# Earlier x loads, a larger planned landing margin and a replanned issue order in a fused attention and feed-forward kernel

## The chip, the cores and the metric

The kernel runs on one core of a Trainium2 chip. The metric is device time in microseconds (us), the median of several executions. The time is 2.2 to 2.3 us more than the span that the profile shows, so differences of spans and differences of times can be compared.

Words used below: TensorE (PE in the profile), ScalarE (ACT), VectorE (DVE), and the queue that sends all DMAs (SPq). A *visit* is one step of the attention part: eight score matmuls, and then two exponentials ("exps") of 128x1024 on ScalarE. There are 512 visits, so 1024 exps.

## The reference, cut to what matters

```python
# B, S, D, H = 1, 2048, 1024, 32; Dh = 32; F = 3584; bf16
def _A_ref(x, wq, wk, wv, wo):
    q = (x @ wq).reshape(B, S, H, Dh).transpose(0, 2, 1, 3)
    k = x @ wk                       # one K and one V head for 32 query heads
    v = x @ wv
    scores = jnp.einsum("bhqd,bkd->bhqk", q, k) * (Dh ** -0.5)
    o = jnp.einsum("bhqk,bkd->bhqd", _softmax(scores), v)
    return o.transpose(0, 2, 1, 3).reshape(B, S, H * Dh) @ wo

def _B_ref(x, w_gate, w_up, w_down):
    return (_sigmoid(x @ w_gate) * (x @ w_up)) @ w_down

h = x + _A_ref(_layernorm(x), wq, wk, wv, wo)
h2 = h + _B_ref(_layernorm(h), w_gate, w_up, w_down)
```

(Shortened from the reference, same arithmetic.)

## The kernel before

The kernel is one Python program that *plans* before it emits. Every instruction becomes an object with an engine, dependencies and an estimated duration; a list scheduler walks through estimated time and appends each object to its engine's list; the lists are then emitted in that order. So a number in the cost estimate changes no instruction's content, only where it stands. An engine takes its list in order, so an instruction whose input is late holds up what stands behind it: in the profile of before, a projection on TensorE that waited 2.37 us held up the scores behind it, and ScalarE then waited 3.15 us for them (both lines are in the prediction).

The parts that the change and the argument touch (cuts marked with `...`):

```python
XT = 1000.0
...
    # Plan.step: when the plan believes that a DMA has landed
    if o.nbytes:
        go = max(s + 1400.0, self.dma_free["sp"])
        self.dma_free["sp"] = go + o.nbytes / 280.0
        o.end = self.dma_free["sp"] + 900.0 + (PIECE if o.key.startswith("sl") else XT if o.key.startswith("xT") else 0.0)
...
    # 65 sets of 5 numbers; visit v uses KNOBS[v // WIN], WIN = 8: which class of work fills TensorE, and when
    KNOBS = [(4, 6, 0, 0, 2), (4, 7, 1, 0, 2), (0, 6, 0, 4, 2), ...]
...
    for ts in [[0], [1]] + [[t, t + 1] for t in range(2, NT, 2)]:      # x tiles of 128 rows, in pairs
        ...                                                           # statistics, then on VectorE:
        xnorm[t] = pl.op("dve", lambda xt=xt, sc=sc: DVE.tensor_scalar(
            out=xt, in0=xt, scalar1=sc, scalar2=None, op0=ALU.mult), [cen, sv[1]], ...)
        if 1 < ts[-1] < NT - 6:
            load_x([ts[-1] + 5, ts[-1] + 6], [xnorm[ts[-1]]])
...
    def dma_xT(t):                                                    # x tiles 2 to 15 are transposed by DMA
        xT_ev[t] = dma(lambda: SP.dma_start_transpose(
            out=xnT4[t // 4][:, :, (t % 4) * P:(t % 4 + 1) * P], in_=x_sb[:, t, :]), f"xT{t}", P * D * 5 // 2,
            [xnorm[t]], prio=0, occ=1330.0)
...
    # emit_S: the two exps of a visit
            exps[u] = pl.op("act", lambda slot=slot, pb=pb: ACT.activation(
                out=pslot(slot).rearrange("p (a b) -> p a b", a=2), in_=S_ps[:, pb:pb + 2, :],
                func=ACTF.Exp, scale=SCALE), [last] + free, prio=3, **t_act(1024))
...
    def flush_hT():                                                   # feed-forward input of row tile t
        while late_hT and (late_hT[0] < 2 or (late_hT[0] - 2) in gu_last):
            t = late_hT.pop(0)
            hT_ev[t] = dma(lambda t=t: SP.dma_start_transpose(
                out=hnT[:, t % 2, :, :], in_=hn[:, :]), f"hT{t % 2}", P * D * 5 // 2,
                [hnorm[t], gu_last.get(t - 2)], prio=0, occ=1330.0)
            ...
...
        # nothing else can start, by the plan: a matmul whose result nobody reads
        pl.op("pe", mm(F_ps[:, spare[0], 0:256], ident[:, :], kT4[:, 0:256], True, True), ...).tag = "dummy"
```

While ScalarE works on the exps, the plan gives TensorE the rest: P times V, the gate and up products (from `hnT`), the down products (from `zone`). The matmul with no reader is called a dummy below.

The softmax here doesn't subtract the row's maximum and nothing guards it: scores larger than these inputs give would overflow.

## Time and profile before

| | before |
|---|---|
| median of 3 runs | 1081.53 us (1080.90 to 1082.35) |
| execution that the profile shows | 1082.78 us, span 1080.5 us |
| exps | 1024, 969.2 us of ScalarE |
| last exp starts, from there to the end | 1014.18, then 66.3 us |

From the page, the engines' busy times and the costliest group (columns: line, engine, operation, out<-in with shapes, count, busy us and mean ns, idle us before and what ended it); then the window of the tail (length, busy us of TensorE, its weight loads, VectorE, ScalarE, GpSimd; clock; DMA share; GB/s):

```profile
PE 1045.8 (97%) x12803; PEld 483.2 (45%) x12972; DVE 902.7 (84%) x1750; ACT 1007.9 (93%) x1172; POOL 28.4 (3%) x58
...
L693 ACT ACTIVATE Pr<-S_ps 128x1024 bf16<-128x1024 f32 x1024 | 969.2, 1179 | 4.7 <-PE S_ps L401 4.5
```

```profile
1010.00:1081.00 71.00, 66.72 (x446) 30.57 (x451) 22.05 (x40) 11.29 (x16) 0.80 (x2) 1.00 0.79 207
```

The exps alone fill 969 of 1080 us, and of all that time only 4.5 us are waits for scores. Two engines with over 90% are no contradiction: TensorE is filled up with feed-forward work that could stand elsewhere, ScalarE cannot give anything away.

### The profile page before, as it was taken

To read this page: it belongs to the slowest core of one execution; us is meant where nothing else is said; L and a number is where in the kernel's file an instruction comes from. 1 tells how busy PE (TensorE), PEld (TensorE's weight loads), DVE (VectorE), ACT (ScalarE), POOL (GpSimd) and SP (SyncE) were. 2 spreads that over 40 slices of the span, in tenths; PEclk is the share of its full clock that TensorE was granted. 3 is DMA by queue.
4 is the path that set the end of the run, shared out by engine and by line. 5 is a ranking of instruction groups with operands and counts; after the bars stand their busy time and mean duration, and the time that the engine had idled before them with its cause. 6 is when DMAs were issued, how large, how long until landed. Compare 5 with 4: busy or idle time off the path is not lost.

```text
span 1080.5 us, 31405 instructions
## 1 busy us (share of the span) xinstructions
PE 1045.8 (97%) x12803; PEld 483.2 (45%) x12972; DVE 902.7 (84%) x1750; ACT 1007.9 (93%) x1172; POOL 28.4 (3%) x58
## 2 busy tenths in 40 slices
PE   9999999999999999999999999999999999999998
PEld 6664444444444444444444444444444444444443
DVE  8789989898988889898888889898898989898721
ACT  6899999999999999999999999999999999999610
POOL 2100000000000000000000000000000000000000
PEclk9999999999999999999999999999999999999999
DMA  9997799927969597939659697987969596876994
GB/s 223 177 300 236 184 290 258 280 66 217 243 174 243 148 277 186 288 85 288 159 142 223 165 280 139 258 201 179 236 151 274 120 279 165 229 201 167 281 269 109
DMA packets 309359, 226.60 MB, mean 210 GB/s; under 512 B 121824, under 2 KB 300512, under 8 KB 309216
## 3 DMA queue, kind: packets, MB, share of 16 engines
q1 hardware_dynamic: 307136, 224.46, 81.3%
q8 instruction: 102, 1.67, 0.7%
q10 hardware_dynamic: 2080, 0.13, 0.1%
q14 instruction: 41, 0.34, 0.1%
HBM read 194.12 MB, written 7.86 MB: 187 GB/s over the span
## 4 chain that ended last, share of the span: by engine, by line
PE 77%; ACT 11%; DVE 5%; issue 5%; DMA 2%; SPq 0%; POOL 0%; DVEq 0%; ACTq 0%
PE F_ps L401 64%; PE S_ps L401 13%; ACT Pr L693 9%; DVE Ts L727 2%; DMA ring<-in_A_x_dram 1%; ACT tnh L968 1%; DVE st L338 1%; DVE st L340 1%; DMA zone<-ring 1%; DVE Rc L786 0%; DVE ring L385 0%; DVE hst L972 0%; DVE hact L287 0%; DVE Ts L734 0%; DVE ring L378 0%
## 5 line engine op out<-in xcount | busy, mean ns | idle before, releaser
L693 ACT ACTIVATE Pr<-S_ps 128x1024 bf16<-128x1024 f32 x1024 | 969.2, 1179 | 4.7 <-PE S_ps L401 4.5
L727 DVE TENSOR_TENSOR Ts<-Ts,Pr 128x1024 bf16<-128x1024 bf16 x736 | 482.5, 677 | 33.6 <-ACT Pr L693 31.7
L401 PE MATMUL F_ps<-ring,hnT 128*128 128x512 bf16 (+1 forms) x2005 | 411.8, 380 | 13.1 <-issue 9.6
L401 PEld LDWEIGHTS F_ps<-ring,hnT 128*128 128x128 bf16 (+1 forms) x2089 | 153.3, 97 | 192.3 <-issue 47.3
L401 PE MATMUL F_ps<-zone,hact 128*128 128x512 bf16 (+1 forms) x1153 | 212.1, 380 | 9.0 <-issue 8.2
L401 PE MATMUL S_ps<-QTb,kT 32*128 32x256 bf16 x4096 | 208.8, 273 | 1.1
L401 PEld LDWEIGHTS S_ps<-QTb,kT 32*128 32x128 bf16 x4096 | 64.1, 92 | 209.1 <-ACT Pr L693 143.5
L401 PE MATMUL F_ps<-Pr,Vb 128*32 128x256 bf16 x4096 | 135.3, 274 | 0.3 <-issue 0.3
L968 ACT ACTIVATE tnh<-F_ps 128x512 f32<-128x512 f32 x112 | 83.0, 742 | 43.1 <-PE F_ps L401 43.0
L401 PEld LDWEIGHTS F_ps<-zone,hact 128*128 128x128 bf16 (+1 forms) x1214 | 80.0, 97 | 92.7 <-issue 22.7
L727 DVE TENSOR_TENSOR Ts<-Pr 128x1024 bf16<-128x1024 bf16 x128 | 87.3, 684 | 39.9 <-ACT Pr L693 39.8
L972 DVE SCALAR_TENSOR_TENSOR hst<-tnh,F_ps 128x512 bf16<-128x512 f32 x112 | 76.6, 684 | 43.9 <-PE F_ps L401 40.8
L401 PEld LDWEIGHTS F_ps<-Pr,Vb 128*32 128x32 bf16 x4096 | 97.6, 96 | 30.2 <-issue 17.6
L401 PE MATMUL F_ps<-zone 128*128 128x256 bf16 (+5 forms) x639 | 74.9, 271 | 4.7 <-DMA zone<-ring 2.4
L401 PE MATMUL F_ps<-wo_sb,OT 128*128 128x512 bf16 (+1 forms) x289 | 61.5, 380 | 1.8 <-issue 1.4
L401 PEld LDWEIGHTS F_ps<-zone 128*128 128x128 bf16 (+1 forms) x646 | 43.6, 98 | 26.9 <-issue 7.6
L734 DVE TENSOR_TENSOR Ts<-Ts 128x1024 bf16<-128x1024 bf16 x64 | 44.0, 688 | 1.3
L1002 DVE SCALAR_TENSOR_TENSOR h_sb<-F_ps,h_sb 128x512 bf16<-128x512 f32 x32 | 21.8, 682 | 22.3 <-PE F_ps L401 22.1
L352 POOL TENSOR_SCALAR zb<-mvb 128x1 bf16<-128x1 bf16 (+1 forms) x25 | 10.3, 411 | 997.9 <-DVE mvb L348 997.9
L401 PEld LDWEIGHTS F_ps<-wo_sb,OT 128*128 128x128 bf16 (+1 forms) x304 | 22.4, 97 | 28.0 <-issue 7.0
L771 DVE COPY Oc<-F_ps 128x256 f32<-128x256 f32 x60 | 25.2, 420 | 7.4 <-PE F_ps L401 6.6
L776 DVE TENSOR_TENSOR Oc<-F_ps,Oc 128x256 f32<-128x256 f32 x60 | 25.4, 423 | 4.8 <-PE F_ps L401 3.2
(60 smaller groups left out, 333.2 us busy)
## 6 DMA issues: line engine op xcount, KB each, us to landing
ring<-in_B_w_gate_dram SPq DMA_DIRECT2D x314, 256.0 KB, 4.3
ring<-in_B_w_up_dram SPq DMA_DIRECT2D x310, 256.0 KB, 4.6
zone<-in_B_w_down_dram SPq DMA_DIRECT2D x28, 256.0 KB, 4.0
h_sb<-in_A_x_dram SPq DMA_DIRECT2D x16, 256.0 KB, 4.8
out_dram<-h_sb SPq DMA_DIRECT2D x32, 128.0 KB, 3.0
ring<-in_A_x_dram SPq DMA_DIRECT2D x7, 512.0 KB, 5.4
QTb<-q_scratch SPq DMA_DIRECT2D x14, 256.0 KB, 4.8
Pr<-in_B_w_up_dram SPq DMA_DIRECT2D x14, 256.0 KB, 4.4
```

What stands on the lines that cost most here:

```text
L338: a = pl.op("dve", lambda k=k, src=src: DVE.bn_stats(st[:, k, 0, :], src[:, 0:512]), dep, prio=prio, occ=590, lat=756, order=[st_user.get(k)])
L340: b = pl.op("dve", lambda k=k, src=src: DVE.bn_stats(st[:, k, 1, :], src[:, 512:1024]), dep, prio=prio, occ=590, lat=756, order=[st_user.g ...
L352: f = pl.op("pool", lambda: POOL.tensor_scalar(out=zb[:, ph, sl].unsqueeze(2), in0=mvb[:, ph, sl, 1:2], scalar1=LN_EPS_BF16, scalar2=None, ...
L401: fn = lambda: PE.matmul(o, lhsT=l, rhs=r, start=start, stop=stop, **kw)
L693: exps[u] = pl.op("act", lambda slot=slot, pb=pb: ACT.activation(out=pslot(slot).rearrange("p (a b) -> p a b", a=2), in_=S_ps[:, pb:pb + 2 ...
L727: o = pl.op("dve", lambda T=T, a=a, b=b: DVE.tensor_tensor(out=T, in0=a, in1=b, op=ALU.add), deps, prio=4, **t_dve(1024, 1.92))
L734: merge_ev[G] = pl.op("dve", lambda T4=T4: DVE.tensor_tensor(out=T4[:, :, 0, :], in0=T4[:, :, 0, :], in1=T4[:, :, 1, :], op=ALU.add), [sum ...
L771: oc_ev[G] = pl.op("dve", lambda: DVE.tensor_copy(out=Oc[:, :], in_=O), [last, o_ev.get(G - 1)], prio=0, **t_dve(256))
L776: a = pl.op("dve", lambda: DVE.tensor_tensor(out=Oc[:, :], in0=O, in1=Ob, op=ALU.add), [last, oc_ev[G], o_ev.get(G - 1)], prio=0, **t_dve( ...
L968: tanh_of[n] = pl.op("act", lambda: ACT.activation(out=tnh[:, n % 2, :], in_=F_ps[:, b, :], func=ACTF.Tanh, scale=0.5), [last, tn_user.get ...
L972: e = pl.op("dve", lambda: DVE.scalar_tensor_tensor(out=hst[:, n % NST, :], in0=tnh[:, n % 2, :], scalar=1.0, in1=F_ps[:, b, :], op0=ALU.a ...
L1002: e = pl.op("dve", lambda: DVE.scalar_tensor_tensor(out=h_sb[:, t % 4, sl], in0=F_ps[:, b, :], scalar=0.5, in1=h_sb[:, t % 4, sl], op0=ALU ...
```

## The change

Its intent: get x tiles 10 to 15 normalized sooner, and make the plan allow more time for the transposes of x to land, so that no projection stands in TensorE's list ahead of its data. The sets of KNOBS are new as well, so the order of work changes all through the kernel.

```diff
-XT = 1000.0
+XT = 1300.0
...
-    KNOBS = [(4, 6, 0, 0, 2), (4, 7, 1, 0, 2), (0, 6, 0, 4, 2), (1, 5, 0, 1, 2), ...
+    KNOBS = [(0, 6, 0, 2, 3), (1, 7, 1, 2, 1), (0, 5, 0, 4, 2), (3, 4, 0, 1, 2), ...
...
-            if 1 < ts[-1] < NT - 6:
-                load_x([ts[-1] + 5, ts[-1] + 6], [xnorm[ts[-1]]])
+            for k in {3: [8, 10], 5: [12], 7: [14]}.get(ts[-1], []):
+                load_x([k, k + 1], [xnorm[ts[-1]]])
```

## The prediction

> **What bounds the kernel now.** I read four things in order: the page, the waits of ScalarE by stretch, the busy time by window, and the timeline around the one large gap.
>
> The page calls TensorE 97% busy and ScalarE 93%. The share that matters is that of each stretch, so next come the windows (columns: stretch, length, busy us of each engine with instruction counts, granted clock, DMA share, GB/s):
>
> ```profile
> 36.00:42.30 6.30, 6.27 (x133) 4.55 (x125) 5.46 (x16) 6.04 (x9) 0.93 (x2) 1.00 1.47 198
> 42.30:47.80 5.50, 3.13 (x42) 2.01 (x39) 3.99 (x14) 2.35 (x4) 0.93 (x2) 0.77 0.84 176
> 47.80:53.00 5.20, 5.20 (x101) 3.79 (x99) 2.90 (x8) 4.86 (x6) 0.00 (x0) 0.92 0.22 47
> 60.00:120.00 60.00, 57.52 (x796) 29.57 (x802) 57.86 (x119) 60.00 (x67) 1.28 (x2) 1.00 0.76 234
> 120.00:1010.00 890.00, 866.08 (x10734) 384.16 (x10886) 777.50 (x1469) 890.00 (x1020) 16.35 (x28) 1.00 0.82 208
> ```
>
> The reader should see: from 60 to 1010 us ScalarE (fourth busy figure) works 950 of 950 us, and its list of waits in that stretch is empty. So the attention part, 1024 exps of 128x1024, is ScalarE without a gap. TensorE fills in feed-forward work there and has 26 us to spare. After the last exp comes a tail of 67 us on TensorE alone. The end is therefore: the moment from which ScalarE no longer waits, plus a fixed pile of ScalarE work, plus the tail. Only the first 60 us have waits of ScalarE to take away. They are (waits of ScalarE, 13 to 60 us: total, times, longest):
>
> ```profile
> ACT Pr L693 <- PE S_ps L401: 4.5, 5, 3.2
> ACT kT L286 <- PE F_ps L401: 1.3, 1, 1.3
> ```
>
> The 3.2 us is one gap. The timeline round it, 41.9 to 48.5 us:
>
> ```profile
> 42.31 0.24 PE L401 MATMUL F_ps<-zone 128*128 128x32 bf16 x3
> ...
> 44.92 2.21 PE L401 MATMUL F_ps<-zone 128*128 128x256 bf16 x25 [2.37 <-DMA zone<-ring]
> ...
> 47.06 0.61 PE L401 MATMUL S_ps<-QTb,kT 32*128 32x256 bf16 x8
> ...
> 47.73 1.02 ACT L693 ACTIVATE Pr<-S_ps 128x1024 bf16<-128x1024 f32 x1 [3.15 <-PE S_ps L401]
> ```
>
> TensorE reaches the K projection of x tiles 10 and 11 at 42.55 us (44.92 less 2.37) and waits for the DMA transposes of these tiles. The scores after them come late, and ScalarE runs dry for 3.15 us. The chain that ended last shows what these transposes hang on:
>
> ```profile
> 24.87 4.29 DMA ring<-in_A_x_dram
> ...
> 35.23 4.08 DMA ring<-in_A_x_dram
> 39.31 5.47 DMA zone<-ring
> 44.92 2.21 PE F_ps L401 x25
> ```
>
> The x load of tiles 14 and 15, sent at 35.23, is in flight in front of the transposes of tiles 10 and 11, sent at 37.92 and 39.31. Those took 6.1 and 5.5 us from issue to landing; the median of all 14 is 3.7.
>
> **What the Trainium skill says.** "Perfetto Trace Analysis", section Optimization Strategy: within a regime, find the gaps on the engine that should be saturated and what they wait for, since a kernel can have several regimes. That is the reading above. The trace agrees that there are regimes: ScalarE 890 of 890 us in the middle, 11 of 71 in the tail.
>
> "TensorE: Matmul & The Clock Gate", section The HAM clock gate: after an idle window of about 3.4 us the array runs at half clock until it has been busy for about as long. The trace agrees in kind: the granted clock is 0.56 between 44.9 and 47.8 us and 0.80 from 47.8 to 50, against 1.00 elsewhere. The gap was shorter (2.37 us) than the page's window, so the number is not borne out. The cost: the 25 matmuls at 44.92 are 8 of 256 columns (0.11 us each), 16 of 32 (0.03) and one more, 1.5 us at full clock, and took about 2.15 (47.06 less 44.92). The wait and the slow clock thus cost about 3 us before the next scores.
>
> "DMA: Bandwidth & Descriptors", section Issuing engines are not separate DMA queues: transfers interleave on the same 16 engines whoever issues them. Nothing in the trace speaks against it: landings of the same transposes range from 3.1 to 6.1 us.
>
> **The change part by part.**
>
> *The loads.* Before, the loads of tiles 8/9, 10/11, 12/13, 14/15 went out at 17.81, 24.87, 29.60, 35.23, each after the normalization of pair 2/3, 4/5, 6/7, 8/9. Now 10/11 follows 8/9 at once (about 18.4, one issue of 0.58 later), and 12/13 and 14/15 take the places at about 24.9 and 29.6. The place at 35.23 is empty. This takes 0.6 us of issue and 512 KB of transfer from in front of the transposes of 10/11. VectorE waited for x four times in that stretch (0.71, 0.38, 0.72, 0.77 us); the last three, 1.9 us, should go. So these transposes should be sent near 36.5 to 37.5 and land by 41 at the median time, by 43 at the worst seen.
>
> *Evacuations.* Comparing the instruction orders, four 256-column evacuations (one of Q, three to hact) pass from ScalarE to VectorE. On ScalarE each holds up the next exp by about 0.27 us (hact at 25.45, exp at 25.72): 1.1 us less there. On VectorE they cost 4 x 0.42 = 1.7 us, about what the earlier loads give it.
>
> *Dummies.* The larger margin makes the plan put 14 dummy matmuls, not 9, before the first projection from DMA transposes (tiles 2/3). That projection did not need even nine: its transposes, sent at 14.53 and 15.9, landed by 19.9 (4.0 us at most) and the dummies ran from 20.05. Five more at 0.11 are 0.55 us of new delay. Ten dummies are new in the whole kernel; the other five (before 6, now 11) are in the stretch where ScalarE is the bound, where 0.5 us of TensorE's 26 spare is free.
>
> *Order.* I summed TensorE's work from the first dummy in both orders, with 0.11 us for 256 columns, 0.0605 for 128, 0.03 for 32, 0.335 for one visit of scores and 1.86 for one PV pair with its sums (all from the timeline). To the end of score visit 11 (from 0): 20.86 us before. The trace has it at 42.31, so the sum plus 20.05 plus 1.40 of small waits. With the same 1.4 to 1.5: the new order ends visit 11 at 43.2 (sum 21.72). The projection of 10/11 now stands behind more Q work: sum 22.38, so 43.9, after the landing even at its worst. Visit 12 ends at 20.05 + 23.60 + 1.5 = 45.15 and its exp starts 0.12 later, at 45.3. Before it was 47.73. **Gain: 2.4 us.** (ScalarE will be waiting then: from the first exp of visit 3, at 23.63 + 0.55, its 18 exps of visits 3 to 11 at 0.93, seven evacuations at 0.27 and some 0.84 of K and V take 19.5 us, to 43.7. So a gap of about 1.6 us remains.)
>
> From there ScalarE needs 1.87 us a visit (9 exps in 8.52 us, 0.934 each). Visits 14 and 15 end at 27.48 and 29.68 in the sum, 2.2 apart, because two PV pairs stand between: about 0.6 us of new gaps there, against 0.25 before. Net **2.1 us**. Projections 12/13 and 14/15 come at sums of 29.68 and 31.36, near 51.3 and 53.1; their transposes should land near 47 and 51.
>
> *The rest.* Before the last exp both kernels have 1024 exps and 102 tanhs on ScalarE, after it ten tanhs. After the last scores TensorE's list is the same, row by row. The new order numbers move feed-forward work about behind ScalarE and cannot shorten it; TensorE's changes of mode are 1043 against 1042. Sum: 1081.5 - 2.1 = **1079.4 us**.
>
> **The rivals.** (a) *The whole stall comes back*: 3.15 us of gap plus the 1.1 us of moved evacuations, less 0.55 of dummies: 3.7 us, 1077.8. For it: the wait is on the chain that ended last, and my 1.4 us of small waits may shrink. Against it: TensorE was busy 6.27 of 6.30 us before the stall, so ScalarE's saved time only shows as its own waiting. (b) *The wait moves*: VectorE, with 1.7 us more to evacuate, normalizes tiles 12 to 15 as late as before (14/15 finished at 50.3) and TensorE waits at 53.1 instead. Before, their transposes landed at 56.6. A stall of 2 to 3 us there gives everything back: 1081.5. Against it: two of VectorE's waits of 47 to 49 us (1.47, 0.71) were consequences of the stall itself, so it should finish near 46 to 48. (c) *The replanned middle opens gaps on ScalarE*: 64 sets of numbers changed. For it: feed-forward groups now stand elsewhere among the score visits. Against it: not one gap in 950 us before. It would cost 1 us or so, 1080.5. (d) *Nothing on the path*: if the small dummies and gaps eat the gain, 1081.5.
>
> **Range and chances.** Rival (a) sets the lower end, at 1077.6 with 0.2 for run scatter; (b) and (d) the upper, 1081.4. The three times of before lie 1.4 us apart, so a median can shift by about 0.5. A change of 2% is 21.6 us; the first 60 us hold only about 6 us of ScalarE waits, and losing 21.6 us would need gaps in a middle that has none. Faster by over 2%: 0.005; slower: 0.01; within: 0.985.
>
> **What would show each step right or wrong.** Right: no wait of TensorE for the transposes near 42 to 45 us, and the clock at 1.00 there; the longest wait of ScalarE for scores near 1.5 to 2 us and not 3.2; visit 12's exp near 45.3; 14 dummies that end after the transposes have landed; ScalarE still 890 of 890 us from 120 to 1010. Wrong: a new wait for transposes at 53 us, a clock below 1 in the first 60 us after the start-up, or any wait of ScalarE after 60 us.

## The result, and the profile after

| | before | after |
|---|---|---|
| median of 4 runs, same chip | 1081.27 us (1080.90 to 1082.35) | 1081.83 us (1081.35 to 1082.98) |
| ratio | | 1.0005 (95%: 0.9988 to 1.0022) |
| profiled execution | 1082.78 us, span 1080.5 | 1081.35 us, span 1079.1 |

A ratio here and below is the mean time of one kernel's fast runs over that of the other's of the same rounds, so it is not quite the ratio of the medians. The time is the same; 1079.4 and the range 1077.6 to 1081.4 were both too low. Note the trap in the last row: the two profiles differ by 1.4 us in favour of after, but before's was a slow execution of its kernel and after's the fastest of its four.

The same windows of after as the prediction shows of before:

```profile
36.00:42.30 6.30, 6.30 (x132) 4.62 (x130) 6.09 (x18) 5.56 (x8) 0.93 (x2) 1.00 0.99 151
42.30:47.80 5.50, 5.50 (x117) 4.00 (x116) 4.26 (x15) 5.47 (x7) 1.32 (x2) 1.00 1.11 184
47.80:53.00 5.20, 5.01 (x140) 3.69 (x128) 1.53 (x3) 4.82 (x7) 0.00 (x0) 1.00 0.78 181
60.00:120.00 60.00, 59.88 (x803) 28.55 (x802) 57.95 (x119) 60.00 (x67) 1.60 (x2) 1.00 0.78 237
120.00:1010.00 890.00, 886.32 (x10846) 384.32 (x10844) 777.19 (x1467) 889.19 (x1019) 15.90 (x28) 1.00 0.80 207
```

In the second row the stall is gone: TensorE 5.50 of 5.50 us (3.13 before), ScalarE 5.47 (2.35 before), clock 1.00 (0.77 before). In the last row ScalarE, whose list of waits had been empty there, is 0.81 us short of 890. (TensorE's larger busy figures are no finding: the trace of before has 12803 matmuls for 12972 weight loads, so 169 records are missing. The second profile of before, told of below, has all of them, and there TensorE is busy 59.00 of 60 and 887.78 of 890 us in the last two rows. So the "26 us to spare" of the prediction are about 3: TensorE too is nearly full, and a late input on it soon reaches ScalarE.) The waits of ScalarE, first from 13 to 60 us, then from 60 to 1010:

```profile
ACT Pr L693 <- PE S_ps L401: 2.0, 5, 0.6
ACT kT L286 <- PE F_ps L401: 1.9, 1, 1.9
```

```profile
ACT Pr L693 <- PE S_ps L401: 0.8, 1, 0.8
```

Waits for scores fell from 4.5 to 2.0 us, the wait for the first projection grew from 1.3 to 1.9 (the added dummies), and one new wait of 0.8 us stands where before had none. The timeline around it in after (start, length, engine, operation, count, what ended the idle time before it):

```profile
162.73 1.04 PE L401 MATMUL F_ps<-ring,hnT 128*128 128x512 bf16 x4
...
165.90 1.30 SPq L877 DMA_TRANSPOSE hnT<-hn  x1
...
168.27 1.06 PE L401 MATMUL F_ps<-Pr,Vb 128*32 128x256 bf16 x32
169.26 0.28 PE L401 MATMUL F_ps<-kT,ident 128*128 128x256 bf16 x1
170.46 0.60 PE L401 MATMUL F_ps<-ring,hnT 128*128 128x512 bf16 x2 [0.93 <-DMA hnT<-hn]
171.00 0.40 PE L401 MATMUL S_ps<-QTb,kT 32*128 32x256 bf16 x8
171.45 1.94 ACT L693 ACTIVATE Pr<-S_ps 128x1024 bf16<-128x1024 f32 x2 [0.81 <-PE S_ps L401]
```

and the same change of row tiles in before:

```profile
168.97 1.23 SPq L877 DMA_TRANSPOSE hnT<-hn  x1
...
169.01 1.25 PE L401 MATMUL F_ps<-ring,hnT 128*128 128x512 bf16 x5
...
173.49 0.28 PE L401 MATMUL F_ps<-kT,ident 128*128 128x256 bf16 x1
173.83 0.38 PE L401 MATMUL F_ps<-ring,hnT 128*128 128x512 bf16 x1
```

`F_ps<-ring,hnT` is gate and up work (L877 sends the transpose). Before, that work of the previous row tile lasts until 170.26; the next tile's transpose is sent at 168.97, lands 3.8 us later at 172.8, and its first matmul at 173.83 waits for nothing. After, the previous tile's gate and up work is used up at 163.8, two us *before* the transpose is sent (165.90). It lands 4.5 us later, at 170.4. Down products, P times V and dummies (`F_ps<-kT,ident`) bridge the 6.7 us between the two tiles, all but 0.93 us, and the scores that stand behind that wait in TensorE's list come 0.81 us late for ScalarE.

One more wait stands in this profile and is easily missed, because the view names another releaser. It is at the projection of x tiles 14 and 15:

```profile
53.28 1.54 PE L401 MATMUL F_ps<-zone 128*128 128x256 bf16 x25 [0.47 <-DVE kT L287]
...
55.20 7.46 ACT L693 ACTIVATE Pr<-S_ps 128x1024 bf16<-128x1024 f32 x8 [0.37 <-PE S_ps L401]
```

The transpose of tile 15 was sent at 48.14 and landed at 53.15, 0.13 us before these matmuls began, and ScalarE waits 0.37 us for the scores behind them. This is rival (b) of the prediction, at the place that it named ("TensorE waits at 53.1 instead").

**A ledger.** Because ScalarE is the bound, the start of its Nth exp is a clock for progress, as long as the same other work lies between two counts (between the 41st and the 171st exp both kernels have ten tanhs). Counting exps in the first profile of each kernel gives:

| start of exp | 7th | 25th | 41st | 171st | last | span |
|---|---|---|---|---|---|---|
| before, us | 23.64 | 47.73 | 63.03 | 187.05 | 1014.18 | 1080.5 |
| after, us | 24.05 | 44.98 | 60.70 | 185.55 | 1012.74 | 1079.1 |
| after less before | +0.4 | -2.75 | -2.3 | -1.5 | -1.4 | -1.4 |

By this table the gain of the first 60 us was 2.3 us (2.1 was predicted), 0.8 was lost again near 171 us, and the rest reached the end. That would be 1.4 us in time. The timed runs show no gain at all. So either part of the table is not typical, or the timed runs hide something.

### The profile page after: what moved, and what is told of

Same layout as the page of the kernel before. It is cut to its first block, busy times and chain, and to the rows that moved or that the text cites. A ratio compares the mean times of both kernels' runs of the same rounds, so it can differ in the third digit from the quotient of the medians.

```text
span 1079.1 us, 31547 instructions
## 1 busy us (share of the span) xinstructions
PE 1068.4 (99%) x12955; PEld 484.4 (45%) x12955; DVE 903.6 (84%) x1754; ACT 1007.3 (93%) x1168; POOL 28.3 (3%) x58
## 4 chain that ended last, share of the span: by engine, by line
PE 93%; ACT 3%; DVE 2%; DMA 2%; issue 1%; SPq 0%
PE F_ps L401 77%; PE S_ps L401 15%; ACT Pr L693 3%; DMA zone<-in_A_wq_dram 1%; DMA zone<-ring 1%; DMA hnT<-hn 0%; DVE st L338 0%; DVE st L340 0%; ACT tnh L968 0%; DVE Ts L727 0%; DVE ring L385 0%; DVE ring L378 0%; SPq L302 0%; DVE mv L342 0%; DVE h_sb L1002 0%
## 5 line engine op out<-in xcount | busy, mean ns | idle before, releaser
L401 PE MATMUL F_ps<-ring,hnT 128*128 128x512 bf16 (+1 forms) x2110 | 428.4, 380 | 3.5 <-issue 2.1
L401 PE MATMUL F_ps<-zone,hact 128*128 128x512 bf16 (+1 forms) x1166 | 223.1, 380 | 0.2 <-issue 0.2
L972 DVE SCALAR_TENSOR_TENSOR hst<-tnh,F_ps 128x512 bf16<-128x512 f32 x112 | 76.4, 682 | 43.3 <-PE F_ps L401 41.7
L401 PE MATMUL F_ps<-zone 128*128 128x256 bf16 (+4 forms) x646 | 74.6, 270 | 1.0 <-DVE kT L287 0.5
L401 PE MATMUL F_ps<-wo_sb,OT 128*128 128x512 bf16 (+1 forms) x304 | 64.7, 380 | 0.0
```

The source lines that it names most:

```text
L401: fn = lambda: PE.matmul(o, lhsT=l, rhs=r, start=start, stop=stop, **kw)
L972: e = pl.op("dve", lambda: DVE.scalar_tensor_tensor(out=hst[:, n % NST, :], in0=tnh[:, n % 2, :], scalar=1.0, in1=F_ps[:, b, :], op0=ALU.a ...
```

## The experiments

First theory (H1): the stall at tiles 10 and 11 is a property of the kernel before, and its gain is given back by the new gap near 171 us and by dummies. Rival (H2): the profile of before shows an unusually bad execution; the usual stall is smaller, so less was ever there to win. Rival (H3): the loads do nothing, the new order does it all.

Experiments edit either kernel as text, or change its finished lists after planning, so that nothing else moves. All 18 runs gave correct results.

### The two kernels once more

No edit. Before (`e1_before_again`), and two looks at it later on another occasion; after (`e1_after_again`, and `e4_after_beside` beside other runs).

> The kernel before, unchanged, for a second profile and more times. Theory A (the profiled execution of before was an unusual one: its span of 1080.5 us is 1.5 us above what its median time leaves; the stall for the transposes of tiles 10/11 is shorter in a usual execution): a span near 1079 us here, and the gap of ScalarE near 45 us well under 3.15 us, at most 1.5 to 2. Theory B (the stall is always there and the new plan gives its gain back later): the gap again 3.0 to 3.3 us and the last exp again near 1015.3 us.

> The changed kernel, unchanged, for a second profile and more times; ratio to before 0.999 to 1.001. Theory A: no stall near 42 to 45 us, ScalarE's waits in the first 60 us about 4 us in all as in the first profile, one gap of about 0.8 us near 165 us at the transpose of the normalized rows. Theory B: gaps of ScalarE after 60 us of 2 us or more in all.

> The changed kernel once more, for comparison on this chip: ratio to before 0.9990 to 1.0010, gap of ScalarE of 0.8 us near 171 us, 25th exp between 44.8 and 46.0 us.

> A third profile of the kernel before, for the stall alone. If the first profile was the odd one: gap of ScalarE near 45 us of 1.2 to 2 us, clock 1.00 there, 25th exp near 46.0. If the two profiles are two equal cases: either is as likely, the 25th exp at 46.0 or at 47.7.

> A fourth profile of the kernel before: as for the third, gap of 1.2 to 2 us and the 25th exp near 46.0 if the first was the odd one.

Times: before again 1081.93 against 1082.07 for before in the same rounds (ratio 0.9998, 0.9986 to 1.0011); after 1082.33 against the same 1082.07 (1.0000, 0.9987 to 1.0012), and 1082.34 against 1081.54 on another occasion (1.0001, 0.9989 to 1.0014). The looks took 1081.67 and 1080.25 (state unknown).

TensorE's wait for tiles 10 and 11 and the exps after it, in the second, third and fourth profile of the same kernel before, one fence each:

```profile
44.06 1.54 PE L401 MATMUL F_ps<-zone 128*128 128x256 bf16 x25 [1.50 <-DVE st L340]
45.98 2.85 ACT L693 ACTIVATE Pr<-S_ps 128x1024 bf16<-128x1024 f32 x3 [1.40 <-PE S_ps L401]
```

```profile
44.74 1.54 PE L401 MATMUL F_ps<-zone 128*128 128x256 bf16 x25 [1.95 <-DMA zone<-ring]
46.67 1.94 ACT L693 ACTIVATE Pr<-S_ps 128x1024 bf16<-128x1024 f32 x2 [1.84 <-PE S_ps L401]
```

```profile
43.30 1.54 PE L401 MATMUL F_ps<-zone 128*128 128x256 bf16 x25 [0.69 <-DVE st L338]
45.23 3.77 ACT L693 ACTIVATE Pr<-S_ps 128x1024 bf16<-128x1024 f32 x4 [0.59 <-PE S_ps L401]
```

The 25 matmuls took 1.54 us each time, so the array was at full speed, against 2.21 us in the first profile. Together (with the start of the Nth exp):

| profile | wait | granted clock, 44 to 48 us | 25th | 41st | 171st | last | span |
|---|---|---|---|---|---|---|---|
| before, first | 2.37 | 0.66 | 47.73 | 63.03 | 187.05 | 1014.18 | 1080.5 |
| before, second | 1.50 | 1.00 | 45.99 | 61.08 | 185.10 | 1012.25 | 1079.5 |
| before, third | 1.95 | 1.00 | 46.67 | 61.76 | 185.79 | 1012.92 | 1079.4 |
| before, fourth | 0.69 | 1.00 | 45.23 | 60.33 | 184.35 | 1011.49 | 1078.0 |
| **mean of before** | 1.63 | | 46.41 | 61.55 | 185.57 | 1012.71 | |
| after, three profiles | none | 1.00 in the first | 44.88 to 45.04 | 60.58 to 60.86 | 185.27 to 185.65 | 1012.46 to 1012.85 | 1078.8 to 1079.2 |
| **mean of after** | 0 | | 44.97 | 60.71 | 185.49 | 1012.68 | |

H2 is right, and H1 is right in its second half. The 25th exp of before lies anywhere between 45.23 and 47.73 us; the first profile is the worst of four. On average the gain at the 25th exp is 1.44 us, at the 41st 0.84. From the 41st to the 171st before took 124.02 us in all four profiles, after 124.85, 124.79 and 124.69: 0.76 lost, in each of the three. ScalarE does the same exps and the same ten tanhs there, busy 124.02 us in before and 124.04 in the first profile of after; the difference is the gap of 0.81. What is left is 0.08 us at the 171st exp and 0.03 at the last: by these means, 0.84 less 0.76 is nothing. The 0.84 rests on four profiles of before with a standard deviation of 1.1 us at the 41st exp, so its standard error is about 0.6 (an estimate from these profiles); the balance says where time was won and lost, not that it is zero to a tenth.

Why only 0.84 of 1.44 reaches the 41st exp can be read from more profiles. The kernels of `e2_hold_wd`, `e3_swap_hT` and `e4_early_norm`, told of below, differ from after only near 160 us and later. In their profiles the transpose of tile 15 lands at 50.6 to 51.4 us, nothing waits at 53 us, and from the 25th to the 41st exp they take 15.14 to 15.15 us. In the three profiles of after it lands at 53.0 to 53.3, TensorE waits 0.46 to 0.59 us, and the same stretch takes 15.71 to 15.83. Before takes 15.09 (15.30 in its first profile). So the wait at 53 us, and hardly anything else, costs these 0.6 us, and it too differs between executions: these three profiles have the 25th exp at 45.91, 45.48 and 44.85 and the 41st at 61.06, 60.62 and 59.99. Over all six the 41st is at 60.63, a gain of 0.9.

The clock tells how common the worst case is. Each run's record has the mean granted clock over the whole span. Both profiles here in which the clock fell near 45 us, this first one and one told of below, show 0.998 there; the other profiles show 1.00. Of 45 runs of before with a recorded clock, 9 have 0.998, and in one set of nine these are the four slowest (1082.69 to 1083.01 against 1080.98 to 1082.27). Of 14 such runs of after, none has. So the prediction was built on an event of about one run in five. (That the other eight fell at the same place was not looked at.) The clock is not the only source of scatter: in another set of nine no run has 0.998, and its slowest, 1083.46 and 1083.70, show 1.00. The profiles show two more. From the start of the last exp to the end it is 66.3 to 66.5 us in most, but 67.2 in the second of before; and from the 171st to the last exp the first profile of `e1_loads_moved`, next, took 827.80 us where two more of the same kernel took 827.14 and 827.18, with no wait in it.

### The loads alone, and the loads undone

`e1_loads_moved` is before, with only the three loads put where the changed kernel has them; all other lists are untouched. `e1_loads_back` is after with the loads put back.

```diff
 # loads_moved, after planning of before
+        rest = []
+        for i, o in enumerate(lists["sp"]):
+            if o is at["x8"]:
+                rest += [at["x8"], at["x10"]]
+            elif i == old["x10"]:
+                rest.append(at["x12"])
+            elif i == old["x12"]:
+                rest.append(at["x14"])
+            elif i != old["x14"]:
+                rest.append(o)
+        lists["sp"] = rest
+        at["x10"].deps, at["x12"].deps, at["x14"].deps = [xnorm[3]], [xnorm[5]], [xnorm[7]]
```

> Before, with only the x loads moved: every other instruction on every engine stands where it stood. Theory A: the transposes of 10/11 land in time; the time falls by what the usual stall costs, 0.5 to 1.5 us, ratio 0.9986 to 0.9995. Theory B: the time falls by 2.5 to 3.7 us, ratio 0.9966 to 0.9977. A third possibility, that the load was not what delayed the transposes: no change, and the stall still there.

> The changed kernel with its x loads put back to the places of before and every other instruction where it stands in the changed kernel. If the loads are what the change lives from: a stall for transposes near 44 us or later returns and the time rises by 1 to 3 us over the changed kernel. If the new order by itself already asks for the transposes late enough (about 1.4 us later than before): no rise, within 0.5 us of the changed kernel.

To see whether what the first run showed holds, two more looks were taken at the first:

> Before with only the loads moved, a second profile. If the load in front delays the transposes: TensorE waits 0.9 us or less for tiles 10/11 and the 25th exp comes by 45.5 us, in this and the next profile. If the wait only varies by execution: it may be anything from 0.7 to 2.4 us, the 25th exp from 45.2 to 47.7.

> A third profile of the same kernel, with the same two readings: wait of 0.9 us or less and the 25th exp by 45.5 us if the load is the cause, anything up to 2.4 and 47.7 if not.

With the loads moved alone, the line that read 2.37, 1.50, 1.95 and 0.69 us of wait reads, in the three profiles:

```profile
43.41 1.54 PE L401 MATMUL F_ps<-zone 128*128 128x256 bf16 x25 [0.67 <-DVE kT L287]
```

```profile
43.27 1.54 PE L401 MATMUL F_ps<-zone 128*128 128x256 bf16 x25 [0.67 <-DVE kT L287]
```

```profile
43.59 1.54 PE L401 MATMUL F_ps<-zone 128*128 128x256 bf16 x25 [0.68 <-DVE kT L287]
```

The wait is 0.67 us three times out of three. (The name behind the arrow is the releaser that the profile saw last; in all seven profiles of the old order the projection starts 0.1 to 0.2 us after the second transpose lands, so that is what it waits for.) The 25th exp is at 45.20 to 45.52, mean 45.35: 1.05 us sooner than the mean of before. Three against four is little, since the fourth profile of before has 0.69 too; but in the 15 profiles with early loads, of whatever kernel, the second transpose landed at 42.8 to 44.2 us, mean 43.3, and in the five with late ones at 43.2 to 45.0, mean 44.3. H3 falls: the loads bring the landing forward by about 1 us, though it still scatters. From the 41st exp to the 171st the kernel takes 124.01 to 124.12 us, as before, so the loads open no gap. The time, 1081.14 against 1082.07, ratio 0.9995 (0.9981 to 1.0008), cannot prove a gain of a thousandth.

Loads back in after: 1084.48 us, ratio 1.0024 (1.0012 to 1.0037), the one clear rise, and the 25th exp at 47.59. I had expected the old wait to return. Another came instead; TensorE's and ScalarE's waits, 13 to 60 us:

```profile
PE F_ps L401 <- DVE hact L287: 1.9, 2, 1.7
```

```profile
ACT hact L286 <- PE F_ps L401: 2.1, 2, 1.6
```

TensorE waits for an evacuation to `hact` by VectorE, and ScalarE for TensorE. The timeline of the same kernel shows what VectorE did:

```profile
29.43 0.69 DVE L338 BATCH_NORM_STATS2 st<-ring 128x6 f32<-128x512 bf16 x1 [1.99 <-DMA ring<-in_A_x_dram]
...
31.37 0.41 DVE L287 CAST hact<-F_ps 128x256 bf16<-128x256 f32 x1
...
31.83 1.05 PE L401 MATMUL F_ps<-zone 128*128 128x256 bf16 x8 [1.66 <-DVE hact L287]
```

VectorE waits 1.99 us for an x load, and the evacuation, one of those that the new order gives it, stands behind the statistics of that tile. So the new order needs the early loads; it is not an alternative to them.

### The dummies

`e2_no_fill` is after without its first group of added dummies, the 14 before the first projection; `e2_moved_no_fill` is before with the loads moved and without its nine; `e4_best_beside` is the same kernel again on another occasion.

```diff
+        fill = [o for o in lists["pe"] if o.tag == "dummy"][20:]
+        at = lists["pe"].index(fill[0])
+        drop = [o for i, o in enumerate(fill) if lists["pe"].index(o) == at + i]
+        lists["pe"] = [o for o in lists["pe"] if o not in drop]
```

> The changed kernel without the 14 dummy matmuls ahead of the first projection from DMA transposes; all else in place. Theory (the dummies only hold TensorE up, since the transposes of tiles 2/3 land by 19.9 us and the dummies end near 21.5): the first exp of visit 3 comes 1.2 to 1.5 us sooner (from 24.05 to about 22.7), and the 41st exp 0.8 to 1.4 us sooner (from 60.70), so 1080.5 to 1081.2 where the changed kernel has 1081.8. Rival (the next wait takes the gain: transposes of 10/11 or VectorE): visit 3 sooner, but the 41st exp at 60.5 or later, no change of the time. A drop of the clock below 1 in the first 40 us would be a third way to lose it.

> Before with the loads moved and without its nine dummies there. Same theory: visit 3 sooner by about 0.9 us; but this order asks for the transposes of 10/11 at 42.5 already and gets them at 43.3, so most of it becomes a longer wait there: 41st exp within 0.3 us of 60.43, time as e1_loads_moved.

> Before with the loads moved and without its nine dummies, the fastest so far, again: 0.9975 to 0.9995 of before, no gap of ScalarE after 60 us, last exp near 1011.5. If its first result was luck: ratio 0.9995 or more.

Without the dummies in after, the 7th exp comes 1.14 us sooner (22.91). Of that 0.2 is left at the 25th (44.78). The 41st is 0.77 sooner (59.93), but 0.57 of it is the wait at 53 us, which this profile does not have, as three with the dummies do not; one of those has its 41st at 59.99. So the dummies held TensorE up, and almost nothing came of their removal. The 171st comes at 185.68, no sooner than in after. TensorE's wait for the transposed `hnT`, and ScalarE's waits after 60 us:

```profile
PE F_ps L401 <- DMA hnT<-hn: 1.2, 1, 1.2
```

```profile
ACT Pr L693 <- PE S_ps L401: 1.4, 2, 1.1
```

The gaps had been 0.8 in all and are now 1.4: what was ahead at the 41st exp was waited for later. Time 1081.88 against 1082.27 (0.9998, 0.9986 to 1.0011).

Before with early loads and without dummies has no gap after 60 us and the earliest last exp of its call, 1011.49. It took 1080.10 us against 1082.27, ratio 0.9980 (0.9968 to 0.9993): the best figure of all, where I had expected that of the loads alone. But its last exp comes no sooner than in the fourth profile of before, also 1011.49. It was not repeated on the other occasion: 1081.15 against 1081.54, 0.9993 (0.9980 to 1.0005), inside the range that I had given for it, but with the last exp at 1013.61. There its profile shows the old trouble:

```profile
44.35 1.79 PE L401 MATMUL F_ps<-zone 128*128 128x256 bf16 x25 [1.90 <-DMA zone<-ring]
```

with a granted clock of 0.64 from 44 to 48 us. Without dummies TensorE reaches the projection a little sooner (44.35 less 1.90 is 42.45 us, against 42.6 to 42.9 with them) and again finds the transposes under way; the second was sent at 39.65, later than in the three profiles with the loads alone (38.60 to 39.10), and landed at 44.22. Two of its ten runs have a mean clock of 0.998.

### The gap near 171 us

Is it the traffic of the down weights, the place of the transpose in the queue, or the moment at which VectorE finishes `hn`? Three edits of after, and the last of them together with the removed dummies:

```diff
 # hold_wd: the next load of down weights waits until hnT has landed
+        first = next(o for o in lists["sp"][at:] if o.key.startswith("wd"))
+        first.deps.append(hT_ev[1])
 # swap_hT: hnT is sent one place sooner in the queue
+        sp[at - 1], sp[at] = sp[at], sp[at - 1]
 # early_norm: VectorE normalizes hn ahead of sums and one product, and the swap
+        lists["dve"] = [o for o in dv[:end] if o not in held_back] + [hnorm[1]] + held_back + dv[end + 1:]
+        sp[at - 1], sp[at] = sp[at], sp[at - 1]
```

> The changed kernel, with the eight weight loads that follow the transpose of the second tile's normalized rows (sent at 165.9 us) held until it has landed. If these loads slow the transpose (4.5 us to landing, median 3.1): it lands by 169.5, the gap of ScalarE of 0.8 us near 171 us goes, the 171st exp comes 0.7 to 0.9 us sooner (from 185.55), and the time falls by 0.5 to 0.9 us. If they do not: gap and time as in the changed kernel.

> The changed kernel, where the transpose of the second tile's normalized rows goes out just before the feed-forward transpose that stood in front of it, not just after. If that neighbour delays it (sent at 164.65 and 165.90, landing 4.4 to 4.8 us after the sending): it lands within 3.6 us, the wait of TensorE for it and the gap of 0.8 us on ScalarE near 171 us go, the 171st exp comes near 184.8 and the time falls by 0.5 to 0.9 us. If it lands no sooner, neither neighbour is the cause and it stays open.

> The changed kernel, where VectorE normalizes the second tile's rows ahead of three exp sums and one feed-forward product that stood before it, and their transpose is sent first. If the wait near 170 us is what takes the gain: the transpose is sent near 164.7 instead of 165.9, ScalarE's gap of 0.8 us goes, the 171st exp comes 0.6 to 0.9 us sooner (near 184.8) and the last exp too (near 1012.0), the time 0.6 to 0.9 us under the changed kernel of this job. If ScalarE loses the time anyway (another wait takes its place): the 171st exp stays near 185.6.

> The same, without the 14 dummies as well. Without them alone the 41st exp came 0.8 us sooner and the 171st not at all. If the wait near 170 us absorbed it: the 171st exp now near 184.0 to 184.4, last exp near 1011.4, time 1.2 to 1.7 us under the changed kernel of this job. If the tile's normalization cannot come sooner still: 171st exp as in e4_early_norm.

Holding the weights back did not help: TensorE waits 1.1 us for `hnT`, which took 4.7 us to land; 1081.97 against 1082.27 (0.9995, 0.9982 to 1.0007). Nor did the place in the queue: 1.1 us, 4.6 us to land; 1081.24 against 1081.40 (0.9997, 0.9984 to 1.0011). The early normalization did: sent at 163.88, landed 3.0 us later. The matmul that had waited 0.93 us, and ScalarE's waits after 60 us:

```profile
169.52 0.59 PE L401 MATMUL F_ps<-ring,hnT 128*128 128x512 bf16 x2
```

```profile
ACT Pr L693 <- PE S_ps L401: 0.2, 1, 0.2
```

So the cause of the gap is shown: the late `hn`. Yet the time stayed, 1081.70 against 1081.54 (0.9997, 0.9985 to 1.0010), and 41st to 171st exp took 124.92 us, no less than in after. (Against the changed kernel of the same occasion, 1082.34, the median is 0.64 us lower, as expected; the ratios to before, 0.9997 and 1.0001, lie well inside each other's intervals.) The waits were split and not removed: TensorE now waits 0.4 us for the product that was held back and 0.7 for another result of VectorE. ScalarE's list of waits hides most of what this costs, because the records of successive exps overlap: they start 0.90 us apart and last 1.0 to 1.3, and idle time is counted only from the end of the last one. Followed by their ends, which are 0.92 us apart where nothing waits, the one late exp of after cost 0.92 us in its first profile and 0.75 in the one of this occasion, and four late ones in the early normalization, at 166.6, 170.5, 174.7 and 176.6 us, cost 0.35, 0.24, 0.05 and 0.12, together 0.76. Without the dummies as well, the 171st exp is at 184.88, 0.8 sooner than without them alone and no sooner than in the early normalization with them (184.92), and TensorE then waits 1.2 and 0.9 us for pieces of the gate and up weights, and the last exp is at 1013.72, later than in after (1012.68): 1081.68 against 1081.54 (0.9997, 0.9984 to 1.0011). Each wait taken away in this order let the next one show.

### Half the new order

`e2_hybrid` has the new KNOBS for the first 64 visits and the old ones after; `e3_hybrid_no_fill` is that without the dummies before the first projection.

```diff
-    KNOBS = <65 new sets>
+    KNOBS = <8 new sets> + <57 old sets, from the 9th on>
```

> The changed kernel up to score visit 63, with the issue numbers of before from visit 64 on. If the new numbers of the middle give 0.8 us back: no gap of ScalarE near 171 us, the 171st exp 0.7 to 0.9 us sooner than in the changed kernel, the time about 0.8 us under it (1081.0). If such gaps come by chance with any replanning: another gap elsewhere after 60 us and no gain.

> The hybrid (changed kernel to score visit 63, numbers of before after it) without the 14 dummies. If the changed early part is worth something once nothing later absorbs it: 0.5 to 1 us under the hybrid, so 1080.0 to 1080.5, level with the best so far. If its middle absorbs it as in the changed kernel: as the hybrid, 1081.0.

The hybrid keeps the early part (41st exp 60.55) and has no wait for `hnT`, but two other gaps of ScalarE after 60 us, 0.7 us in all (it has two tanhs fewer than after between the 41st and the 171st exp, so its 171st is no measure); 1081.02 against 1082.27, 0.9987 (0.9974 to 1.0001). Its sister has none after 60 us, the last exp at 1011.51 and 1080.16 us against 1081.40, 0.9993 (0.9980 to 1.0005). Both point to a gain of about a thousandth; neither interval excludes 1.

## Why the prediction was wrong

Point by point, by its own steps.

- *"Only the first 60 us have waits of ScalarE to take away."* Right of before. In all four profiles of before the stretch from the 171st exp to the last took 827.1 us, and 827.2 in after.
- *The loads let the transposes of tiles 10 and 11 land in time, and the wait and the slow clock vanish.* Right in the end: no wait in three profiles of after, and the loads alone cut it to 0.67 us, three times. But the second transpose was expected by 41 us, "by 43 at the worst seen", and landed at 43.15, 43.23 and 42.80. The wait is gone because the new order asks later: in the first profile the projection begins at 43.56, 0.4 us after the landing (43.9 was predicted). The margin was thin, and partly luck.
- *Visit 12's exp at 45.3.* It came 0.3 to 0.4 us sooner: the 25th exp started at 44.88 to 45.04. The 1.6 us for which ScalarE was to wait there were 0.03; in the first profile its longest wait for scores is 0.6, before the 21st exp.
- *"14 dummies ... 0.55 us."* Right: the wait for the first projection grew from 1.3 to 1.9 us. That "TensorE's 26 spare" made further work there free was a reading of missing records; it had about 3.
- **"Before it was 47.73. Gain: 2.4 us."** This is the first step that failed. 47.73 is right for the profile and wrong for the kernel, whose mean of four profiles is 46.41. The gain that the other arithmetic gives is 1.44 us there and 0.84 at the 41st exp, where "net 2.1" stood. The prediction saw that the landings of the same transposes range from 3.1 to 6.1 us, and that the wait hung on two of the slowest of them; it did not draw the conclusion that such a wait differs from run to run.
- **"...their transposes should land near 47 and 51", and the "0.6 us of new gaps" of visits 14 and 15.** This is the second step that failed. Those gaps hardly showed: where nothing waits at 53 us, the 25th to the 41st exp takes 0.05 us more than before, not 0.35. The transpose of tile 15 landed at 53.0 to 53.3 in the three profiles of after, and the wait for it cost 0.6. That is rival (b), smaller than its "2 to 3 us" and for another reason: VectorE had normalized the tile by 45.9 at the latest, but its transpose was sent at 48.1 to 48.3, since the issue of the one before it took 2.2 to 2.6 us on the queue, and landed 4.9 to 5.0 us later. In the three profiles without the wait that issue took 1.2 us and the landing 3.5 to 3.6. Why they differ is open.
- **"The new order numbers move feed-forward work about behind ScalarE and cannot shorten it."** This is the third step that failed. The new order opened one gap of 0.8 us near 171 us, in every profile of after. Rival (c) had named this, at "1 us or so", and said what would show it: "any wait of ScalarE after 60 us". It was given too little weight, because the middle of before was free of gaps and I took that as a property of the kernel and not of that one order, and because TensorE seemed to have 26 us to spare.
- *Time.* Predicted net gain 2.1 us. With the mean in place of one profile 1.44 at visit 12; less 0.6 for rival (b), 0.84; less 0.76 for rival (c), 0.08 us, which agrees with the timed runs within their scatter.

Open remain: why the transpose of `hn` takes 4.5 to 4.7 us in this order where the median of all landings of `hn` in after is 3.1 (less traffic of down weights did not shorten it), why that of tile 15 is sent and lands so late in some executions, and whether any version here is faster than before by a thousandth.

## What to carry to other kernels

A wait that hangs on the landing of a DMA has a distribution, and one profile is one draw from it: before a gain is computed from such a wait, compare the profiled execution with the median of the timed runs and profile the old kernel two or three times more. When a replanned order is judged, follow the bound engine by counting its instructions (25th, 41st, 171st, last): the count shows where time was won and lost to a tenth of a us, while end times scatter by one or two. A new order of a full machine has thin places of its own, and a gain at the start must survive each of them. Afterwards, look in the new profile for the sign of each rival that was named: that of (b) stood at 53 us under the name of another releaser, and only the landing time of the transpose gave it away.

## What the Trainium skill lacked or had wrong

- "TensorE: Matmul & The Clock Gate", section The HAM clock gate, puts half clock after at least one idle window of about 3.4 us. Here the granted clock fell to 0.66 and 0.64 (mean of 44 to 48 us) after waits of 2.37 and 1.90 us, and stayed at 1.00 after waits of 1.95 and 1.50. So a shorter gap can trip it, and its length alone does not decide. The page's free-running window fits: both times the clock was at half for 3.41 us, and in these traces its changes lie whole multiples of 3.41 us apart. On that grid the waits of 2.37, 1.90 and 1.50 us each fell into one window, while that of 1.95 us was cut into 0.98 and 0.96. So a window need not be idle throughout; an estimate from these four is that between 1.5 and 1.9 us of idle time in one window is enough. (The prediction said that the page's number was not borne out; its length of the window is.)
- "DMA: Bandwidth & Descriptors", section DMA Transpose (X-bar), gives the constraints of a transpose (and another section an effective rate), but no time from issue to landing beside other transfers. For one 128x1024 tile of bf16 these runs show 3.0 to 6.1 us, and that spread, not the mean, decided the stall.
- "Perfetto Trace Analysis", section Optimization Strategy, starts from the gaps of one trace and does not say that a gap may differ between executions. The same wait was 2.37, 1.50, 1.95 and 0.69 us in four profiles of one kernel, and the exp behind it started between 45.23 and 47.73 us.
